# Moving a modulation product to GpSimd and casts ahead of a gelu in a one-core adaLN block

## The chip, the core and the metric

The kernel runs on one core of a Trainium2 chip. A core has five engines with queues of their own: TensorE (PE) multiplies matrices and writes to PSUM; VectorE (DVE) reduces and does arithmetic; ScalarE (ACT) applies functions; GpSimd (POOL) does arithmetic in SBUF; SyncE (SP) issues most DMAs. Each queue runs in the order in which it was written, and an instruction that waits holds up all behind it. The metric is the device time of one execution in microseconds (us).

## The reference

One transformer block for 2048 tokens of width 448 with 16 heads of width 28, in float32. A condition vector `c` gives six rows by one product: shift, scale and gate of the attention half (sa, ca, ga) and of the feed-forward half (sb, cb, gb).

```python
mod = (_silu(c) @ w_mod).reshape(c.shape[0], 6, 1, -1)
sa, ca, ga, sb, cb, gb = (mod[:, 0], mod[:, 1], mod[:, 2], mod[:, 3], mod[:, 4], mod[:, 5])
h = _layernorm(x, axis=-1) * (1 + ca) + sa
x = x + ga * _A_ref(h, A_wqkv, A_wo)      # softmax attention, 16 heads
h = _layernorm(x, axis=-1) * (1 + cb) + sb
x = x + gb * _B_ref(h, B_w1, B_b1, B_w2, B_b2)   # layernorm, 448 -> 1792, gelu, 1792 -> 448
return x
```

`w_mod` has 448 rows and 2688 columns, six parts of 448. The first part of the product below means sa and ca, the second ga, sb, cb and gb.

## The kernel before

**Numbers as two parts.** Most matrix products split each operand into a rounded part (`hi`, type fp32r) and the rest (`lo`), and add three products. Getting the pair takes a cast and a subtraction.

**Three stages.** The *projections* (to about 168 us) form Q, K and V for four blocks (`b`) of 512 tokens, normalise the next block meanwhile, and take the first row maxima of the attention scores. *Attention* runs 16 units: four head groups `g` of four heads by four query blocks `qt`, unit `u = 4 g + qt`. A unit has 16 steps, one for each 128 keys, and a step is 12 score matmuls (line 1382), two exponentials of 128 x 1024 on ACT (line 1395) and four matmuls with V of the step before (line 1337). The *feed-forward* part runs 14 steps `i` for each of four blocks, each with 11 matmuls of the first layer, a gelu, the split of its result, and 12 matmuls of the second layer for the step two back (`LAG`).

**Row maxima.** Before a unit begins, the maximum of each score row over all keys must be known. Single matmuls (line 476) put 128 x 512 scores in PSUM, and DVE reduces them (line 481). They are woven into the steps of earlier units by a plan made when the program is built. Before step `RING` = 121 a step has 3 to 5 such matmuls. From there on a step has one single, in the PSUM tile called `m1`, and one pair in a tile of two banks that DVE reduces at once (line 686). Before step 121 maxima over two key blocks can also be paired in another way: POOL forms the difference of two K blocks (`make_kd`, tile `d0h`); at the end of an odd step `open_pair` multiplies by it, ACT applies Relu, and in the next step `close_pair` adds the scores of the first block and takes the maximum in one DVE operation. `load_hi` loads a K or Q block of the next head group as soon as the last maximum that reads the old one is planned. When both blocks of a pair are issued, it plans `make_kd` for four steps later, and pairs may open from one step after that.

**The second part of the modulation.** `mod_load` brings four chunks of `w_mod` (128 or 64 rows, 1792 columns) into the slots of V blocks 2 and 3; `mod_mm` multiplies each by silu(c), broadcast to 32 columns, in block 1's first four projection tasks (line 752), so that each of the four rows lies 32 times in one PSUM tile. `mod_fin` copies it with three ACT operations, adds 1 to the third quarter (cb), sends four rows to DRAM and reads each back, broadcast to 128 partitions. The row ga scales `wo`, whose preparation (`wo_prep`, five items) runs at steps 0 to 16; the first product with it stands at step 216.

**The end of a unit.** `unit_end_tasks` sends the denominators through DRAM, multiplies on POOL (line 1062), casts `hi` (line 1072, DVE for 13 units), subtracts on POOL (line 1073) and stores both parts in DRAM. `max_fin` closes a set of maxima; POOL clears 16 columns of its tile each time (line 517).

**Seams of the feed-forward part.** Between blocks the rows of the next block, turned through DRAM (`send`, `fetch`), are cast to `hi` by ACT (line 1192) and subtracted by DVE (line 1193), four chunks each. They are written behind the whole first-layer step `i` = 13, that is behind its gelu (line 1428), the split of its result and two weight items. The seven tiles of a block rotate over eight buffers.

Of the kernel before, what the change touches and what calls it, by code (L numbers as in the profile page):

```python
# [13 lines left out]
F32 = mybir.dt.float32  # L14
# [8 lines left out]
D = 448  # L23
H = 16
DH = 28
# [7 lines left out]
P1RATE = 4  # L33
LAST_MAX = NKT - 4
RING = 121
PAIR_AT = (2, 2, 0, 2)
PAIR_ROWS = {(0, 2): 2, (0, 3): 3, (1, 0): 2, (1, 1): 2, (1, 2): 3}
WO_MAX = 3
# [6 lines left out]
def tile_adaln_block(ctx: ExitStack, tc: tile.TileContext, x, wqkv, wo, w1, b1, w2, b2, c, w_mod, out):  # L45
# [33 lines left out]
    def sbt(tag, shape, dt=F32, bufs=1):  # L79
        return sb.tile(shape, dt, tag=tag, name=nm(tag), bufs=bufs)  # L80
# [40 lines left out]

    ident = sbt("ident", [128, 128])
    make_identity(nc, ident)
    cst = sbt("cst", [128, 5])
    neg_half, zero_col = cst[:, 0:4], cst[:, 4:5]
    pool.memset(neg_half, -0.5)
    pool.memset(zero_col, 0.0)


    cols = sbt("cols", [128, 2 * NC])  # L130
# [183 lines left out]
    pc = ps_o()  # L314
    pe.transpose(pc[:, :NC], c_rows, ident[:NC, :NC])
    act.activation(sil_b, pc[:, :NC, None].broadcast_to([128, NC, 32]), AF.Silu)
    warm_up(5)
    for k in range(NC):
        for j in range(2):
# [183 lines left out]
    def load_hi(kind, g, b):  # L503
        loaded[(kind, g, b)] = clock[0] + (5 if clock[0] >= RING else 3)
        tg = ("kh" if kind else "qh") + str(b)
        t = sb.tile([128, 512], F32R, tag=tg, name=nm(tg), bufs=1)
        (kh_sb if kind else qh_sb)[(g, b)] = t
        sp.dma_start(f(t), f(dscr[kind][0][g])[:, b * 512 : (b + 1) * 512])
        if kind and b in (PAIR_AT[g], PAIR_AT[g] + 1) and all((g, PAIR_AT[g] + c) in kh_sb for c in range(2)):
            at(clock[0] + 4, lambda: make_kd(g))  # L510

    late = []


    def max_fin(g, qt):
        m32 = sbt("m32", [128, 32], F32R, bufs=2)
        pool.memset(f(m32)[:, 16:32], 0.0)
        dve.tensor_reduce(
            out=m32[:, 0:16].rearrange("p (h i) -> p h i", i=4),
            in_=mxp[(g, qt)].rearrange("p i h c -> p h i c"), op=ALU.max, axis=AX.X, negate=True,  # L520
        )
# [217 lines left out]

    mod = {}  # L740

    def mod_load(k):
        mod[k] = slot(f"v{2 + k % 2}", [128, 4 * D], F32)
        load_mod(mod[k], k, 2 * D, 4)

    def mod_mm(k):
        if k == 0:
            mod["p"] = ps_o()
        p = mod["p"]
        for j in range(4):  # L750
            rs_, cs = mod_part(k, j, 4)
            pe.matmul(
                p[32 * j : 32 * j + 32, :D], sil_b[rs_, k, :], mod[k][rs_, cs],
                start=(k == 0), stop=(k == NC - 1),
            )

    def mod_fin():
        t = sbt("full", [128, 512], bufs=3)
        act.copy(t[0:64, :D], mod["p"][0:64, :D])
        act.activation(t[64:96, :D], mod["p"][64:96, :D], AF.Identity, bias=1.0)  # L760
        act.copy(t[96:128, :D], mod["p"][96:128, :D])
# [56 lines left out]
    for b in range(NB):  # L818
# [12 lines left out]
        for n, (tb, kind, g) in enumerate(tasks):  # L831
# [41 lines left out]
                    later[n - 7](None)  # L873
            if n == (4 if b else 6):
                v_init(b)
            if b == 0 and n == 6:
                mod_load(0)
                mod_load(1)
# [4 lines left out]
            if b == 1:  # L883
                if n < 2:
                    mod_mm(n)
                    mod_load(2 + n)
                elif n in (2, 3):
                    mod_mm(n)
                    if n == 3:
                        mod_fin()  # L890
            if not more:
                if n == 0:
                    load_q(0)
# [68 lines left out]
    def wo_item(n):  # L962
# [11 lines left out]
        def go(r):  # L974
            full = sbt("full", [128, 512], bufs=3)
            ps = slice(0, 112 if n == 3 else 128)
            pool.tensor_tensor(out=full[ps, :D], in0=r[ps, :D], in1=rows["ga"][ps], op=ALU.mult)

            def rest():
                if n == 3:  # L980
                    hi = sbt("hi", [128, 512], F32R, bufs=3)
                    dve.tensor_copy(hi[ps, :D], full[ps, :D])
                    pool.tensor_tensor(out=wo_p[1][ps, 2, :], in0=full[ps, :D], in1=f(hi)[ps, :D], op=ALU.subtract)
                    pool.tensor_copy(wo_p[1][0:32, 2, :], f(hi)[0:32, :D])
# [6 lines left out]
            at(6 + 2 * n, rest)  # L991

        return ld, go

# [44 lines left out]
    def unit_end_tasks(u, o_sb):  # L1039
# [24 lines left out]
        def t_split2():  # L1064
# [7 lines left out]
            (dve.tensor_copy if staged else act.copy)(hi, on)  # L1072
            pool.tensor_tensor(out=lo, in0=on, in1=f(hi), op=ALU.subtract)
            st["hi"], st["lo"] = hi, lo
            if staged:
# [176 lines left out]
        sched.setdefault(step, []).append(fn)  # L1252

    wo_prep = Prep([wo_item(n) for n in range(5)])
    at(0, lambda: wo_prep.load(2))
    for n in range(5):
        at(4 + 2 * n, wo_prep.step)

    def b2_load():
        rows["b2"] = raw_t()  # L1260
# [13 lines left out]
        at(1 + i, lambda: put_spare(1))  # L1274
    for g in (1, 2):
        at(6 + g, lambda g=g: put_ones(g))
    at(15, b2_load)
    at(28, b2_mul)
    last0 = NKT * (NU - 1)
    lnst = [ln2_stages(b) for b in range(NB)]  # L1280
    for i in range(14):
# [133 lines left out]

    ov = out[0].rearrange("(b p t) n -> b p t n", p=128, t=4)

    def mlp1(b, i):
# [37 lines left out]
    def mlp2(b, m):  # L1456
# [18 lines left out]
        if m == NFT - 1:  # L1475
            for t in range(4):
                ot = xn_t()
                dve.tensor_tensor(out=ot[:, :D], in0=om[b][t][:, :D], in1=acc[b][:, t, :], op=ALU.add)
                sp.dma_start(ov[b][:, t, :], ot[:, :D])

    seq = [(b, i) for b in range(NB) for i in range(NFT)]
    for n in range(len(seq) + LAG):
        if n < len(seq):
            b, i = seq[n]
            if n:
                mlp1(b, i)
            for fn in tail.pop(n, ()):
                fn()
            for _ in range(2 if n % 2 else 1):
# [2 lines left out]
                lnst[b + 1][0](i)  # L1492
            if b:
                lnst[b][0](20 + i)
        ahead = n < len(seq) and i == NFT - 1 and b + 1 < NB
        if ahead:
            for k in range(2):
                lnst[b + 1][1](k)
        if n >= LAG:
            mlp2(*seq[n - LAG])  # L1500
        if ahead:
            for k in range(2, NC):
                lnst[b + 1][1](k)
    for key in ("t3", "t2", "t1", "t0", "m2", "m1", "o"):
        ps_close(key)

# [34 lines left out]
```

## Time and profile before

| | us |
|---|---|
| median of 3 runs | 1099.84 (1099.55 to 1100.01) |
| the profiled execution, its own time | 1099.75 |
| its span, from the first to the last instruction | 1097.5 |
| projections, to the first exponential of attention | 167.2 |
| a unit of attention, units 1 to 6 | 40 |
| a unit of attention, units 8 to 12 | 36 |
| a loop step of the feed-forward part | 5.0 |

A profile row gives start and duration in us, engine, line, operation, output and inputs, and in brackets the engine's idle time before it with what ended it. Rows of the grouped view give count, busy time in all, and the mean in ns. `PEld` is TensorE's weight load. Matmul ends are modelled, so starts are safer to compare than durations. The granted TensorE clock was 1.000 throughout.

### The profile page before, as it was taken

Reading aid. Unit: us, or ns where it says so; the run is one execution under the profiler, and the core shown is the slowest. Engines: PE = TensorE matmul, PEld = TensorE weight load, DVE = VectorE, ACT = ScalarE, POOL = GpSimd, SP = SyncE. Lnnn points to the kernel's source line nnn. Section 1 sums busy time; section 2 is a strip of 40 time slices with the busy share of each in tenths; the row PEclk is TensorE's granted clock in tenths of the full one; section 3 lists DMA queues with packets and bytes.
Section 4 is the critical chain, followed back from the end, with each engine's and each line's share of the span. In section 5 each row is a group of like instructions: output and inputs, shape, how many; then the busy total and the mean of one; then the engine's idle time right before and its main releaser. Section 6 shows DMA issues by size and latency. Waiting matters only on the chain.

```text
span 1097.5 us, 20709 instructions
## 1 busy us (share of the span) xinstructions
PE 1088.1 (99%) x8255; PEld 658.3 (60%) x8255; DVE 805.1 (73%) x1382; ACT 697.6 (64%) x883; POOL 198.7 (18%) x201
## 2 busy tenths in 40 slices
PE   8999999999999999999999999999999999999998
PEld 6756675444444444444444444554488788888887
DVE  6968788999999999988888888575655565463322
ACT  4565667888888888888888888678933411211211
POOL 1543332210000000000000000217123042061000
PEclk9999999999999999999999999999999999999999
DMA  9563354121222201232211213111442302002000
GB/s 312 207 190 103 97 188 134 59 65 32 72 76 64 77 28 41 67 98 54 69 48 38 86 49 104 58 31 59 136 137 65 101 34 55 18 34 72 34 1 34
DMA packets 58438, 88.57 MB, mean 81 GB/s; under 512 B 13759, under 2 KB 25686, under 8 KB 58330
## 3 DMA queue, kind: packets, MB, share of 16 engines
q1 hardware_dynamic: 57858, 86.51, 26.3%
q8 instruction: 65, 1.06, 0.4%
q10 hardware_dynamic: 148, 0.46, 0.1%
q0 software_dynamic: 336, 0.28, 0.1%
q14 instruction: 31, 0.25, 0.1%
HBM read 59.39 MB, written 29.50 MB: 81 GB/s over the span
## 4 chain that ended last, share of the span: by engine, by line
PE 96%; DVE 2%; DMA 1%; ACT 1%; issue 0%; SPq 0%; DVEq 0%; ACTq 0%
PE s L1382 23%; PE o L1337 23%; PE m L396 16%; PE pa L396 9%; PE m L476 8%; PE s L1472 3%; PE s L1473 3%; PE s L1474 3%; PE s L476 2%; PE t L1473 1%; PE t L1474 1%; PE t L1472 1%; DVE y L1193 1%; DMA slot_c<-in_w_mod_dram 1%; PE o L277 1%; DVE mxp L481 0%
## 5 line engine op out<-in xcount | busy, mean ns | idle before, releaser
L481 DVE TENSOR_REDUCE mxp<-m 128x1 f32<-128x512 f32 x555 | 359.7, 685 | 65.0 <-PE m L476 49.6
L1382 PE MATMUL s<-slot_b,slot_a 28*128 28x512 f32 (+1 forms) x3072 | 356.7, 423 | 0.0
L1382 PEld LDWEIGHTS s<-slot_b,slot_a 28*128 28x128 f32 (+1 forms) x3072 | 211.1, 183 | 176.0 <-ACT slot_c L1395 96.4
L476 PE MATMUL m<-kh,qh 28*128 28x512 f32 x607 | 226.9, 468 | 0.5 <-DVE mxp L481 0.3
L1395 ACT ACTIVATE slot_c<-s 128x1024 f32<-128x1024 f32 x170 | 174.7, 1028 | 51.6 <-PE s L1382 50.8
L1337 PE MATMUL o<-slot_c,v 128*32 128x512 f32 x680 | 178.9, 605 | 0.0
L1428 ACT ACTIVATE full<-m,b_col 128x512 f32<-128x512 f32 x56 | 38.6, 689 | 206.6 <-PE m L396 201.4
L686 DVE TENSOR_REDUCE mxp<-s 128x2 f32<-128x1024 f32 x107 | 131.1, 1226 | 5.1
L1337 PE MATMUL o<-slot_c1h,v 128*32 128x512 f32 x512 | 134.7, 605 | 0.0
L1337 PE MATMUL o<-slot_c0h,v 128*32 128x512 f32 x508 | 133.6, 605 | 0.0
L1395 ACT ACTIVATE slot_c1h<-s 128x1024 f32<-128x1024 f32 x128 | 130.7, 1021 | 0.0
L1395 ACT ACTIVATE slot_c0h<-s 128x1024 f32<-128x1024 f32 x127 | 130.5, 1028 | 0.0
L1395 ACT ACTIVATE slot_d<-s 128x1024 f32<-128x1024 f32 x86 | 88.4, 1028 | 25.0 <-PE s L1382 24.7
L1431 DVE CAST hi<-full 128x512 fp32r<-128x512 f32 x42 | 18.7, 444 | 112.3 <-ACT full L1428 112.3
L476 PEld LDWEIGHTS m<-kh,qh 28*128 28x128 f32 x607 | 90.7, 182 | 15.2 <-DVE mxp L481 13.1
L1337 PE MATMUL o<-slot_d,v 128*32 128x512 f32 x344 | 90.5, 605 | 0.4 <-ACT osb L1301 0.4
L1062 POOL TENSOR_TENSOR osb<-osb,osb 128x512 f32<-128x512 f32 x16 | 20.6, 1286 | 362.8 <-DMA osb<-drec 343.5
L1432 DVE TENSOR_TENSOR lo<-full,hi 128x512 fp32r<-128x512 f32 x56 | 46.0, 822 | 29.7 <-ACT hi L1431 25.1
L396 PE MATMUL m<-y,slot_a 128*128 128x512 f32 x160 | 60.9, 397 | 0.4 <-DVE y L1193 0.2
L481 DVE TENSOR_REDUCE mxp<-ma 128x1 f32<-128x512 f32 x61 | 39.5, 681 | 13.2 <-PE m L476 9.2
L1337 PEld LDWEIGHTS o<-slot_c,v 128*32 128x32 f32 x680 | 24.5, 108 | 39.1 <-issue 36.5
L650 DVE CUSTOM_DVE_ANT_0 slot_d0i<-m,slot_d0i 128x512 f32<-128x512 f32 x54 | 37.3, 691 | 14.3 <-PE m L476 11.3
(351 smaller groups left out, 1824.2 us busy)
## 6 DMA issues: line engine op xcount, KB each, us to landing
slot_b<-d SPq DMA_DIRECT2D x32, 256.0 KB
slot_a<-d SPq DMA_DIRECT2D x32, 256.0 KB
d<-lo SPq DMA_DIRECT2D x28, 256.0 KB
d<-hi SPq DMA_DIRECT2D x16, 256.0 KB
osb<-drec SPq DMA_DIRECT2D x15, 256.0 KB
out_dram<-xn SPq DMA_DIRECT2D x16, 224.0 KB
raw<-in_B_w_dram SPq DMA_DIRECT2D x14, 224.0 KB
qh<-d SPq DMA_DIRECT2D x12, 256.0 KB
```

What stands on the lines that cost most here:

```text
L396: pe.matmul(p, a, b, start=(i == 0), stop=(i == len(terms) - 1))
L476: pe.matmul(m, qh_sb[(g, qt)][js, i * 128 : (i + 1) * 128], k[js, :], start=True, stop=True)
L481: dve.tensor_reduce(out=mxp[(g, qt)][:, i, j, cch : cch + 1], in_=m, op=ALU.max, axis=AX.X)
L686: dve.tensor_reduce(out=mxp[(g, qt)][:, i, j : j + 2, cch], in_=t, op=ALU.max, axis=AX.X)
L1337: pe.matmul(o[32 * j : 32 * j + 32, :], v_sb[kt // 4][:, kt % 4, 4 * g + j, :], p[j // 2][:, j % 2, :], start=(kt == 0), stop=(kt == NKT - 1),
L1382: pe.matmul(s2[:, jj, :], ks[rows_, kp, kc], qs[rows_, qp, :], start=(term == 0), stop=(term == 2))
L1395: act.activation(pt[hf], s2, AF.Exp, scale=SCALE)
L1428: act.activation(gf, p, AF.Gelu_apprx_tanh, bias=b1_col[:, i : i + 1])
L1432: dve.tensor_tensor(out=glo, in0=gf, in1=f(ghi), op=ALU.subtract)
L1472: pe.matmul(pp, ghi[:, ts], w_hi, start=(m == 0), stop=False)
L1473: pe.matmul(pp, ghi[:, ts], w_lo, start=False, stop=False)
L1474: pe.matmul(pp, glo[:, ts], w_hi, start=False, stop=(m == NFT - 1))
```

## The change

Five edits.

1. The second part of the modulation leaves the projections. From step 124 on, every five steps, a chunk of 896 columns of `w_mod` is loaded into slot `a2h`; two steps later POOL multiplies it by silu(c) as a column (`sil_c`) and, from the second chunk on, adds it to a running sum, in `b1h` for ga and sb and in `a3h` for cb and gb. At step 166 four matmuls with a column of ones sum over the partitions, and one ACT operation adds 1 to the third quarter through a bias column (`third`).
2. `wo_prep` moves from steps 0 to 16 to steps 174 to 188, and the preparation of b2 with it.
3. The `hi` cast at the end of 13 units goes from DVE to POOL.
4. `make_kd` is planned one step after the second load, no longer four. The tiles of `max_fin` are made and cleared once.
5. At a seam the four casts and subtractions stand between the matmuls and the gelu of step `i` = 13.

```diff
-            at(clock[0] + 4, lambda: make_kd(g))
+            at(clock[0] + 1, lambda: make_kd(g))
...
+    m32s = [sbt(f"m32_{i}", [128, 32], F32R) for i in range(2)]
+    for m32 in m32s:
+        pool.memset(f(m32)[:, 16:32], 0.0)
...
-    def mod_load(k):
-        mod[k] = slot(f"v{2 + k % 2}", [128, 4 * D], F32)
-        load_mod(mod[k], k, 2 * D, 4)
...
-    def mod_mm(k):
...
+    def mod_load(h, k):
+        rs_ = mod_rows(h, k)
+        mod["raw"] = slot("a2h", [128, 2 * D], F32)
+        c0 = 2 * D * (1 + h)
+        sp.dma_start(mod["raw"][rs_], w_mod[128 * k : min(128 * k + 128, D), c0 : c0 + 2 * D])
+
+    def mod_add(h, k):
...
+        col = sil_c[rs_, k : k + 1].broadcast_to([rs_.stop - rs_.start, 2 * D])
+        pool.tensor_tensor(out=raw if k else total, in0=raw, in1=col, op=ALU.mult)
+        if k:
+            pool.tensor_tensor(out=total, in0=total, in1=raw, op=ALU.add)
+
+    def mod_fin():
+        p = ps_mx()
+        ones_ = v_sb[0].rearrange("p t h d -> p (t h) d")[:, 0:32, DH]
         for j in range(4):
...
+                p[32 * j : 32 * j + 32, :D], ones_, mod[j // 2][:, j % 2 * D : (j % 2 + 1) * D], start=True, stop=True,
...
+        act.activation(t[:, :D], p[:, :D], AF.Identity, bias=third)
...
-            (dve.tensor_copy if staged else act.copy)(hi, on)
+            (pool.tensor_copy if staged else act.copy)(hi, on)
...
-    at(0, lambda: wo_prep.load(2))
+    for i in range(2 * NC):
+        h, k = divmod(i, NC)
+        at(MOD_AT + 5 * i, lambda h=h, k=k: mod_load(h, k))
+        at(MOD_AT + 5 * i + 2, lambda h=h, k=k: mod_add(h, k))
+    at(MOD_AT + 10 * NC + 2, mod_fin)
+    at(WO_AT - 4, lambda: wo_prep.load(2))
...
         mm_acc(p, [(w, y) for y, w in ts])
+        if mid:
+            mid()
...
+    def seam(b):
+        return lambda: [lnst[b][1](k) for k in range(NC)]
...
-                mlp1(b, i)
+                mlp1(b, i, seam(b + 1) if i == NFT - 1 and b + 1 < NB else None)
```

The built programs show how this moves instructions. First PE in the projections, block 1, around the first modulation group (`pa` is a projection's PSUM tile, `o` the modulation's, `m` a row maximum's). Before:

```order
L396 MATMUL pa_742<-slot_c0h_511,slot_a_19_124 128x512
L396 MATMUL pa_742<-slot_c0h_511,slot_a_18_123 128x512
L752 MATMUL o_761<-slot_v_116_523,slot_d_4_86 32x448 x4
L396 MATMUL pa_774<-slot_c_110_510,slot_a_20_125 128x512
L396 MATMUL pa_774<-slot_c_110_510,slot_a_22_127 128x512
```

With the change:

```order
L401 MATMUL pa_745<-slot_c0h_518,slot_a_20_126 128x512
L401 MATMUL pa_745<-slot_c0h_518,slot_a_19_125 128x512
L401 MATMUL pa_770<-slot_c_113_517,slot_a_21_127 128x512
L401 MATMUL pa_770<-slot_c_113_517,slot_a_23_129 128x512
L401 MATMUL pa_770<-slot_c0h_518,slot_a2h_128 128x512
```

The group between two projection tasks is gone, here and at three later tasks. Its successor stands on PE in unit 10, between the V matmuls of step 165 (`o`) and the scores of step 167 (`s`), with the change:

```order
L1346 MATMUL o_7765<-slot_c1h_7901,v_233 32x512 x2
L1346 MATMUL o_7765<-slot_d_1903_7900,v_233 32x512 x2
L772 MATMUL m_1915_7958<-slot_b1h_6666,v_232 32x448 x2
L772 MATMUL m_1915_7958<-slot_a3h_7318,v_232 32x448 x2
L1391 MATMUL s_1923_7976<-slot_b_1768_7280,slot_a_1583_6431 128x512 x2
L481 MATMUL m_1924_7979<-kh_1804_7426,qh_1375_5591 128x512
```

The four matmuls of line 772 write a tile of the kind that the row maximum of line 481, two score matmuls later, writes again. Last, ACT at the first seam, from the gelu of step `i` = 12 on (`full<-m` is a gelu, `y` a cast of the next block's rows, `slot_e` a weight cast). Before:

```order
L1428 ACTIVATE full_11624<-m_2696_11612,b_col_253 128x512
L1431 CAST hi_11626<-full_11624 128x512
L1242 CAST slot_e_2700_11630<-full_11631 128x448
L1428 ACTIVATE full_11659<-m_2702_11647,b_col_253 128x512
L1431 CAST hi_11661<-full_11659 128x512
L1242 CAST slot_e_2700_11630<-full_11665 128x448
L1192 CAST y_11669<-xn_11591 128x4x4x32
L1192 CAST y_11670<-xn_11593 128x4x4x32
L1192 CAST y_11671<-xn_11595 128x4x4x32
L1192 CAST y_11675<-xn_11597 128x4x4x32
```

With the change:

```order
L1439 ACTIVATE full_11609<-m_2690_11597,b_col_260 128x512
L1442 CAST hi_11611<-full_11609 128x512
L1246 CAST slot_e_2694_11615<-full_11616 128x448
L1196 CAST y_11644<-xn_11576 128x4x4x32
L1196 CAST y_11645<-xn_11578 128x4x4x32
L1196 CAST y_11646<-xn_11580 128x4x4x32
L1196 CAST y_11650<-xn_11582 128x4x4x32
L1439 ACTIVATE full_11659<-m_2696_11632,b_col_260 128x512
L1442 CAST hi_11661<-full_11659 128x512
L1246 CAST slot_e_2694_11615<-full_11665 128x448
```

The four casts have passed the last gelu, its cast and a weight cast. The subtractions on DVE pass the split of that gelu's result in the same way.

More of the change, by code (lines that the diff above doesn't have):

```diff
@@ L35 @@
 RING = 121
+MOD_AT = 124
+WO_AT = 178
 PAIR_AT = (2, 2, 0, 2)
@@ L123, in tile_adaln_block @@
     make_identity(nc, ident)
-    cst = sbt("cst", [128, 5])
-    neg_half, zero_col = cst[:, 0:4], cst[:, 4:5]
+    cst = sbt("cst", [128, 6])
+    neg_half, zero_col, third = cst[:, 0:4], cst[:, 4:5], cst[:, 5:6]
     pool.memset(neg_half, -0.5)
-    pool.memset(zero_col, 0.0)
+    pool.memset(cst[:, 4:6], 0.0)
+    pool.memset(third[64:96], 1.0)
+    sil_c = sbt("sil_c", [128, NC])
     cols = sbt("cols", [128, 2 * NC])
@@ L316, in tile_adaln_block @@
     act.activation(sil_b, pc[:, :NC, None].broadcast_to([128, NC, 32]), AF.Silu)
+    act.activation(sil_c, pc[:, :NC], AF.Silu)
     warm_up(5)
@@ L509, in load_hi @@
         if kind and b in (PAIR_AT[g], PAIR_AT[g] + 1) and all((g, PAIR_AT[g] + c) in kh_sb for c in range(2)):
-            at(clock[0] + 4, lambda: make_kd(g))
+            at(clock[0] + 1, lambda: make_kd(g))
     late = []
+    m32s = [sbt(f"m32_{i}", [128, 32], F32R) for i in range(2)]
+    for m32 in m32s:
+        pool.memset(f(m32)[:, 16:32], 0.0)
     def max_fin(g, qt):
-        m32 = sbt("m32", [128, 32], F32R, bufs=2)
-        pool.memset(f(m32)[:, 16:32], 0.0)
+        m32s.append(m32s.pop(0))
+        m32 = m32s[-1]
         dve.tensor_reduce(
@@ L989, in rest @@
                     pool.tensor_tensor(out=wo_p[1][:, k, :], in0=full[:, :D], in1=f(wo_p[0])[:, k, :], op=ALU.subtract)
-            at(6 + 2 * n, rest)
+            at(WO_AT + 2 + 2 * n, rest)
         return ld, go
@@ L1254, in tile_adaln_block @@
     wo_prep = Prep([wo_item(n) for n in range(5)])
-    at(0, lambda: wo_prep.load(2))
+    for i in range(2 * NC):
[4 more added lines that the diff above has]
+    at(WO_AT - 4, lambda: wo_prep.load(2))
     for n in range(5):
-        at(4 + 2 * n, wo_prep.step)
+        at(WO_AT + 2 * n, wo_prep.step)
     def b2_load():
@@ L1276, in tile_adaln_block @@
         at(6 + g, lambda g=g: put_ones(g))
-    at(15, b2_load)
-    at(28, b2_mul)
+    at(WO_AT + 11, b2_load)
+    at(WO_AT + 24, b2_mul)
     last0 = NKT * (NU - 1)
@@ L1494, in tile_adaln_block @@
                 lnst[b][0](20 + i)
[L1495 to L1498, printed above, removed]
         if n >= LAG:
             mlp2(*seq[n - LAG])
-        if ahead:
-            for k in range(2, NC):
-                lnst[b + 1][1](k)
     for key in ("t3", "t2", "t1", "t0", "m2", "m1", "o"):
```

27 lines of the change are left out of this document (6 added, 21 removed).

## The prediction

> **What bounds the kernel now.** First the page's busy line and its chain of waits:
>
> ```profile
> PE 1088.1 (99%) x8255; PEld 658.3 (60%) x8255; DVE 805.1 (73%) x1382; ACT 697.6 (64%) x883; POOL 198.7 (18%) x201
> PE 96%; DVE 2%; DMA 1%; ACT 1%; issue 0%; SPq 0%; DVEq 0%; ACTq 0%
> ```
>
> TensorE (PE) is busy 99% and holds 96% of the chain that ended last. So an edit counts by the PE work that it adds or removes, and by the few places where PE waits. Then the view by windows (busy time of PE, weight loads, VectorE (DVE), ScalarE (ACT) and GpSimd (POOL) in a stretch, with the instructions of each; then clock, DMA share, GB/s):
>
> ```profile
> 60.00:75.00 15.00, 15.00 (x83) 8.45 (x80) 11.06 (x21) 8.59 (x17) 3.61 (x4) 1.00 0.73 226
> 209.00:249.00 40.00, 40.00 (x385) 18.42 (x381) 36.59 (x70) 33.91 (x39) 5.01 (x5) 1.00 0.26 73
> 488.00:524.00 36.00, 36.00 (x372) 15.58 (x368) 31.30 (x37) 31.52 (x34) 2.62 (x3) 1.00 0.22 62
> ```
>
> PE has no gap, neither in the projections (first row) nor in attention, whose units take about 40 us before step 121 and 36 us after it (second and third row). There DVE and ACT are near it, at 31 of 36 us or more: work put on them is not free. POOL has 33 of 36 us left.
>
> **Term 1: the modulation matmuls leave the projections.** The timeline shows four groups at line 752; here are the first and the last, each with PE's next work:
>
> ```profile
> 57.34 0.96 PE L752 MATMUL o<-slot_v,slot_d 128*32 128x448 f32 x8
> 58.23 1.20 PE L396 MATMUL pa<-slot_c,slot_a 128*128 128x512 f32 x4
> 71.89 0.96 PE L752 MATMUL o<-slot_v,slot_d 64*32 64x448 f32 x8
> 72.78 1.21 PE L396 MATMUL pa<-slot_c,slot_a 128*128 128x512 f32 x4
> ```
>
> Each group holds PE for 58.23 - 57.34 = 72.78 - 71.89 = 0.89 us, so 4 x 0.89 = 3.56 us go. Can DVE, which takes the row maxima behind PE, follow? Its first reduction behind each group, with its idle time in brackets:
>
> ```profile
> 60.11 1.89 DVE L481 TENSOR_REDUCE mxp<-m 128x1 f32<-128x512 f32 x3 [5.09 <-PE ma L476]
> 66.66 0.69 DVE L481 TENSOR_REDUCE mxp<-ma 128x1 f32<-128x512 f32 x1 [2.25 <-PE m L476]
> 69.53 1.29 DVE L481 TENSOR_REDUCE mxp<-ma 128x1 f32<-128x512 f32 x2 [0.38 <-PE m L476]
> 76.11 0.69 DVE L481 TENSOR_REDUCE mxp<-m 128x1 f32<-128x512 f32 x1 [2.29 <-PE ma L476]
> ```
>
> Behind the first, second and fourth group DVE was idle for longer than 0.89 us, so PE can come that much earlier; behind the third it had only 0.38 us to give. I take 3 x 0.89 + 0.38 = **-3.0 us**. Bounds: -1.9, if a third of it meets PSUM buffers that DVE has not emptied, and -4.0, if ScalarE, which loses three copies there, was holding PE too.
>
> **Term 2: the same sum inside attention.** It takes eight loads (steps 124 to 159), then on POOL eight multiplications and six additions of 896 columns, and at step 166 four matmuls and one ScalarE pass. The nearest rows:
>
> ```profile
> L1062 POOL TENSOR_TENSOR osb<-osb,osb 128x512 f32<-128x512 f32 x16 | 20.6, 1286 | 362.8 <-DMA osb<-drec 343.5 <-ACT slot_d L1395 19.4
> L1124 POOL TENSOR_TENSOR xn<-xn,row_cb 128x448 f32<-128x448 f32 x16 | 19.6, 1225 | 21.8 <-DVE xn L217 20.1 <-PE m L396 1.7
> 202.53 0.55 POOL L984 CAST slot_e<-hi 32x448 fp32r<-32x448 f32 x1
> L458 ACT COPY v<-pa 128x448 f32<-128x448 f32 x15 | 8.0, 534 | 3.6 <-PE pa L396 3.6
> ```
>
> 896 columns are twice 448, so an operation is 2.45 us and a stage at most 4.9 us. Stages come every 5 steps of 36/16 = 2.25 us, which is 11.25 us; a unit end's own three operations (1.29 + 0.63 for the cast, scaled from 448 to 512 columns, + 1.29 = 3.2 us) fit in as well. The last load is issued at step 159 and the matmuls stand at 166, 15.75 us later; with some 5 us for the load (an estimate: 0.23 MB, at the 62 GB/s and more of these stretches) and 4.9 us on POOL about 6 us are spare, so PE does not wait for the sum. PE pays 0.89 us for four matmuls like a group of line 752, and up to 0.5 us because the next row maximum needs the same PSUM tile (m1), which the ScalarE pass (0.53 us) must have read. I take **+1.2 us**; bounds +0.5 (DVE and ScalarE, on which PE leans here, catch up meanwhile) and +2.0 (the pass queues behind a whole exponential).
>
> The preparation of wo, now at steps 174 to 188, is first needed at step 216. Its five DVE casts fall where unit-end casts of the same size leave DVE: 0, and up to +0.5 us if each delays a maximum.
>
> **Term 3: unit-end cast and K difference, nothing.** The cast stood in line on DVE, and POOL waited for it:
>
> ```profile
> POOL lo L1073 <- DVE hi L1072: 93.1, 12, 9.7
> 242.69 0.82 SPq L508 DMA_DIRECT2D kh<-d  x2
> 247.22 1.28 POOL L611 TENSOR_TENSOR slot_d0h<-kh,kh 128x512 fp32r<-128x512 f32 x1 [6.03 <-PE s L1382]
> 248.06 0.50 PE L1382 MATMUL s<-slot_b,slot_a 29*128 29x512 f32 x2
> ```
>
> No unit waits for its result, which goes to DRAM; what hides the move is POOL's idle time. The K difference only moves which maxima are paired: 55 pairs for 54, with as many matmuls in nearly every step. Its risk is a difference that comes late, since PE opens the first pair of head group 1 at the end of step 31 instead of 35, and everything on PE queues behind it. The difference was ready at 247.22 + 1.28 = 248.50, and PE came to step 32 at 248.06: 0.4 us short. But the load stood behind the unit end's stores on SP's queue, and these leave earlier once POOL need not wait for the cast. I take 0; bounds 0 and +0.6.
>
> **Term 4: the seams.** In the chain, the first-layer matmuls of the feed-forward part start at:
>
> ```profile
> 865.56 2.56 PE m L396 x11
> 870.56 2.58 PE m L396 x11
> 882.74 2.56 PE m L396 x11
> 942.95 2.58 PE m L396 x11
> 953.34 2.56 PE m L396 x11
> 1013.57 2.58 PE m L396 x11
> 1023.96 2.55 PE m L396 x11
> ```
>
> A loop step is 870.56 - 865.56 = 5.00 us. Across the three seams two steps take 12.18, 10.39 and 10.39 us instead of 10.0 to 10.02: 2.16 + 0.37 + 0.37 = 2.9 us lost. The casts of the next block's rows stand behind the last gelu, its own cast and a weight cast. The change puts them ahead, where ScalarE is idle until that gelu's matmuls end; each new tile takes the buffer of an old one that these matmuls have just left, so the last cast ends about when they do. The gelu's result is wanted by PE two groups later, so a short delay of it costs nothing. At the first seam the rows' fetch may hold the casts:
>
> ```profile
> 869.08 2.42 SPq L1152 DMA_DIRECT2D xn<-y_dr  x5
> 874.00:874.50 0.50, 0.50 (x4) 0.47 (x3) 0.00 (x0) 0.50 (x1) 0.00 (x0) 1.00 0.28 82
> 874.50:875.00 0.50, 0.50 (x4) 0.46 (x3) 0.46 (x1) 0.01 (x1) 0.00 (x0) 1.00 0.00 0
> 876.27 2.18 ACT L1192 CAST y<-xn 128x512 fp32r<-128x512 f32 x4
> 876.94 0.50 PE L396 MATMUL m<-y,slot_b 128*128 128x512 f32 x1 [1.36 <-ACT y L1192]
> ```
>
> The DMA engines fall silent before 874.5, and PE wants the first tile at 870.56 + 5.00 = 875.6. I take **-2.7 us**; bounds -2.9, and -0.7 if the rows could not be used before 876.27, where the casts began.
>
> **Sum.** -3.0 + 1.2 + 0 - 2.7 = -4.5 us. The profiled execution took 1099.75 us, of which 1097.5 are the span, and the median of the runs is 1099.84: I predict **1095.3 us**.
>
> **Rivals.**
> 1. *The maxima hold the projections* (15%). DVE and five PSUM tiles set the pace, and term 1 gives only 0.4. For it speaks the 0.38 us of idle time behind the third group, against it the 2.25 and 2.29 us behind others. 1095.3 + 2.6 = 1097.9.
> 2. *The seam's rows are late* (9%). The first seam gives 2.0 less: 1097.3. For it speaks that only 1.1 us lie between silent DMA engines and PE's need, against it that the tiles land one after another.
> 3. *POOL blocks DVE in units 7 to 10* (9%); this is the slower end. In the feed-forward part a DVE subtraction from SBUF takes 1.46 us beside a POOL operation, and 0.69 alone:
>
> ```profile
> 901.73 1.46 DVE L1432 TENSOR_TENSOR lo<-full,hi 128x512 fp32r<-128x512 f32 x1
> 941.85 0.69 DVE L1432 TENSOR_TENSOR lo<-full,hi 128x512 fp32r<-128x512 f32 x1
> 541.32 1.30 POOL L1062 TENSOR_TENSOR osb<-osb,osb 128x512 f32<-128x512 f32 x1 [25.34 <-DMA osb<-drec]
> 541.47 0.69 DVE L481 TENSOR_REDUCE mxp<-m 128x1 f32<-128x512 f32 x1 [0.24 <-PE m L476]
> 542.20 0.22 DVE L518 TENSOR_REDUCE m<-mxp 128x16 fp32r<-128x64 f32 x1
> 542.33 1.22 DVE L686 TENSOR_REDUCE mxp<-s 128x2 f32<-128x1024 f32 x1
> ```
>
> In each of some 3.3 units DVE has four small operations from SBUF (a reciprocal, a memset, a reduction, a transposition). One could wait up to 2.45 us, less the 2.25 - 1.22 - 0.69 = 0.34 us that a step leaves, and POOL works 4.9 of 11.25 us: 3.3 x 4 x 2.1 x 0.44 = 12 us, so 1107. It decides from about 0.4 us of blocking on. Against it: beside POOL both the maxima, which read PSUM, and the small reduction kept their lengths. The Trainium skill (SBUF — State Buffer, "SBUF: two separate sides") states that GpSimd and a VectorE operation in a two-port mode or with two SBUF inputs take one pair of ports as an exclusive lock. The subtraction's rows agree with that rule; by it the maxima go free, and the sum stays.
> 4. *POOL's sum is late for its matmuls* (3%). If load and sums take 10 us longer than worked out, PE waits 4: 1099.3. Only the POOL time that was scaled up speaks for it.
>
> **Chances and range.** The forecast has 64%. Measurements of this kernel tell about 0.2% (2.2 us) from no change, so faster means under 1097.6 and slower over 1102.0. The forecast (but for 0.01), and some two thirds of the second and half of the first rival are faster, which makes 0.77; the rest of these and the fourth are no change, 0.14; the third is slower, 0.09. The bounds of the terms add up to -4.0 + 0.5 - 2.9 = -6.4 us at the good end, and -1.9 + 2.0 + 0.5 + 0.6 - 0.7 = +0.5 at the bad one, which needs all at once; I cut it where the first two rivals are inside: 1093.3 to 1098.6.
>
> **What would show it.** Right: no modulation matmuls between 57 and 72 us and attention beginning some 3 us earlier; attention units still of 40.0 and 36.0 us, but once 1 to 1.5 us more in unit 10; two loop steps of about 10.0 us over each seam. Wrong: projections as long as before, longer units 7 to 10, a wait of PE at step 31 or 166, or first-layer matmuls that still wait for the casts.

## The result and the profile after

The changed kernel takes **1094.09 us** (median of 4 runs, 1093.38 to 1094.88), the kernel before 1099.92 beside it: a ratio of 0.9944, with a 95% interval of 0.9932 to 0.9956. The forecast was 1095.3 us (1093.3 to 1098.6). The profiled execution took 1094.19 us, of which 1092.4 are the span, 5.1 less than before. Measured once more, later, the kernel gave 1094.13 us beside 1100.74, a ratio of 0.9942 (0.9929 to 0.9955).

Lines have new numbers: single maxima stand at line 481 (476 before), their reduction at 486 (481), the scores at 1391 (1382), the exponentials at 1404 (1395), the first layer of the feed-forward part at 401 (396). First the page's busy line and its chain of waits, of the changed kernel:

```profile
PE 1083.7 (99%) x8231; PEld 658.3 (60%) x8231; DVE 800.6 (73%) x1369; ACT 697.1 (64%) x883; POOL 231.9 (21%) x215
PE 96%; DMA 2%; DVE 1%; ACT 1%; issue 0%; SPq 0%; ACTq 0%
```

PE lost 4.4 us of work and is as full as before. POOL does 33 us more, VectorE has the thirteen casts less. What PE waited for (in all, times, longest, in us), the first row before:

```profile
PE m L396 <- ACT y L1192: 1.4, 1, 1.4
```

and the longest row of this kind that is new after:

```profile
PE m L481 <- ACT full L776: 0.3, 1, 0.3
```

PE's longest wait, the seam's, is gone from these rows, and a short new one stands behind the modulation's ScalarE pass in unit 10.

**Stages.** Since PE is busy 99% of the span, the lengths of the stages tell where the time went. A unit is measured from its first exponential to the next unit's, in the timeline of ScalarE. For unit 10, before:

```profile
559.92 1.02 ACT L1395 ACTIVATE slot_c<-s 128x1024 f32<-128x1024 f32 x1 [0.33 <-PE s L1382]
595.87 1.02 ACT L1395 ACTIVATE slot_c<-s 128x1024 f32<-128x1024 f32 x1 [0.35 <-PE s L1382]
```

and after:

```profile
555.99 1.03 ACT L1404 ACTIVATE slot_c<-s 128x1024 f32<-128x1024 f32 x1 [0.35 <-PE s L1391]
593.30 1.03 ACT L1404 ACTIVATE slot_c<-s 128x1024 f32<-128x1024 f32 x1 [0.30 <-PE s L1391]
```

595.87 - 559.92 = 35.95 us have become 593.30 - 555.99 = 37.31. All stages in that way; a seam is the two loop steps over it, and the projections run from block 1's first matmul to the first exponential:

| stage | before | after | difference | forecast | after, second profile |
|---|---|---|---|---|---|
| projections from block 1 | 118.25 | 114.84 | -3.41 | -3.0 | 114.77 |
| units 1 to 7 | 279.08 | 278.47 | -0.61 | 0 | 278.60 |
| units 8 and 9 | 71.94 | 71.99 | +0.05 | 0 | 72.01 |
| unit 10 | 35.95 | 37.31 | +1.36 | +1.2 | 37.34 |
| units 11 to 13 | 117.22 | 117.47 | +0.25 | 0 | 117.32 |
| unit 14 | 44.70 | 44.07 | -0.63 | 0 | 44.07 |
| first seam | 12.18 | 10.58 | -1.60 | -2.0 | 10.24 |
| second and third seam | 20.76 | 19.98 | -0.78 | -0.7 | 19.98 |
| behind the third seam | 73.71 | 73.93 | +0.22 | 0 | 73.86 |

These add up to -5.15; what lies ahead of block 1, unit 0, unit 15 and the steps between the seams moved by 0.07 us or less each. The rows below tell how each came about.

**Projections.** The first reductions behind the places where the groups stood, in VectorE's timeline, which answer to the four rows of the prediction:

```profile
59.08 1.89 DVE L486 TENSOR_REDUCE mxp<-m 128x1 f32<-128x512 f32 x3 [3.98 <-PE m L481]
64.78 0.69 DVE L486 TENSOR_REDUCE mxp<-ma 128x1 f32<-128x512 f32 x1 [1.42 <-PE m L481]
67.19 1.28 DVE L486 TENSOR_REDUCE mxp<-ma 128x1 f32<-128x512 f32 x2
72.83 0.69 DVE L486 TENSOR_REDUCE mxp<-m 128x1 f32<-128x512 f32 x1 [1.36 <-PE ma L481]
```

VectorE's idle time went from 5.09 to 3.98, from 2.25 to 1.42, from 0.38 to none and from 2.29 to 1.36: 1.11 + 0.83 + 0.38 + 0.93 = 3.25 us. What was to be given was given, and behind the third group VectorE is now the one that PE cannot outrun.

**Unit 10.** PE, ScalarE and VectorE around the modulation's matmuls:

```profile
570.63 0.55 PE L772 MATMUL m<-slot_b1h,v 128*32 128x448 f32 x2
571.50 0.50 PE L1391 MATMUL s<-slot_b,slot_a 29*128 29x512 f32 x2
571.63 0.63 ACT L776 ACTIVATE full<-m,cst 128x448 f32<-128x448 f32 x1 [0.22 <-PE m L772]
572.32 0.49 PE L481 MATMUL m<-kh,qh 28*128 28x512 f32 x1 [0.32 <-ACT full L776]
572.85 0.69 DVE L486 TENSOR_REDUCE mxp<-m 128x1 f32<-128x512 f32 x1 [1.92 <-PE m L481]
```

Four matmuls hold PE for 571.50 - 570.63 = 0.87 us; the single maximum of step 167 then waits for the ScalarE pass that reads its tile. VectorE meanwhile has no maxima for 1.92 us.

**POOL in units 7 to 10.** A multiplication of the sum (line 764) and its last addition (line 766):

```profile
503.29 1.68 POOL L764 TENSOR_TENSOR slot_a2h<-slot_a2h,sil_c 128x896 f32<-128x896 f32 x1 [11.28 <-DMA slot_a2h<-in_w_mod_dram]
...
556.87 2.12 POOL L766 TENSOR_TENSOR slot_a3h<-slot_a3h,slot_a2h 64x896 f32<-64x896 f32 x1
```

The sum is done at 558.99, 11.6 us ahead of its matmuls. And what VectorE did in 480 to 575 us meanwhile, grouped (count, busy us, mean ns, idle before); before:

```profile
L481 DVE TENSOR_REDUCE mxp<-m 128x1 f32<-128x512 f32 x42 | 29.0, 691 | 10.4 <-PE m L476 9.5 <-PE s L1382 0.6
L518 DVE TENSOR_REDUCE m<-mxp 128x16 fp32r<-128x64 f32 x2 | 0.4, 220 | 0.1
```

and after:

```profile
L486 DVE TENSOR_REDUCE mxp<-m 128x1 f32<-128x512 f32 x41 | 28.3, 691 | 12.3 <-PE m L481 10.9 <-PE s L1391 1.2
L525 DVE TENSOR_REDUCE m<-mxp 128x16 fp32r<-128x64 f32 x2 | 0.4, 220 | 0.1
```

No mean moved by a nanosecond, here or in the small operations left out: POOL's work takes nothing from VectorE here. Of the small operations that VectorE does on SBUF, a reduction of 0.22 us at 488.77 and a transposition of 0.20 us at 523.57 ran beside a multiplication of 896 columns (488.14 to 489.82 and 522.60 to 524.28) and kept their lengths; no reciprocal met one, so for that one this run shows nothing.

**First seam.** In the profiled execution PE still met late rows; ScalarE's casts, and the first matmul of step 13 and of the next block's step 1:

```profile
867.45 0.39 PE L401 MATMUL m<-y,slot_c 128*128 128x512 f32 x1
870.57 1.24 ACT L1196 CAST y<-xn 128x512 fp32r<-128x512 f32 x2 [1.34 <-DMA xn<-y_dr]
872.93 1.14 ACT L1196 CAST y<-xn 128x512 fp32r<-128x512 f32 x2 [1.12 <-DMA xn<-y_dr]
878.03 0.40 PE L401 MATMUL m<-y,slot_b 128*128 128x512 f32 x1
```

The casts no longer queue behind the gelu; two of them now wait for the fetched rows, 1.34 and 1.12 us, and the two steps take 878.03 - 867.45 = 10.58 us. The other two seams take 9.99 each.

### The profile page after: what moved, and what is told of

The parts are those of the page before. It is cut to its first block, busy times and chain, and to the rows that moved or that the text cites. A ratio compares the mean times of both kernels' runs of the same rounds, so it can differ in the third digit from the quotient of the medians.

```text
span 1092.4 us, 20666 instructions
## 1 busy us (share of the span) xinstructions
PE 1083.7 (99%) x8231; PEld 658.3 (60%) x8231; DVE 800.6 (73%) x1369; ACT 697.1 (64%) x883; POOL 231.9 (21%) x215
## 4 chain that ended last, share of the span: by engine, by line
PE 96%; DMA 2%; DVE 1%; ACT 1%; issue 0%; SPq 0%; ACTq 0%
PE o L1346 23%; PE s L1391 23%; PE m L401 16%; PE pa L401 9%; PE m L481 8%; PE s L1483 3%; PE s L1484 3%; PE s L1485 3%; PE s L481 2%; PE t L1484 1%; PE t L1485 1%; PE t L1483 1%; DMA slot_c<-in_w_mod_dram 1%; PE o L281 1%; DMA y_dr<-slot_e 1%; PE ma L481 0%
```

## The experiments

Ratios are to runs of the kernel before on the same chip in the same session, whose medians were 1100.49 (first four kernels), 1100.64 (next four) and 1100.74 us (last three). Differences of a few tenths are below what a ratio's interval resolves; there the lengths of stages decide, which among the profiles of kernels with the same work in a stage agree within about 0.2 us.

**1. The seams alone**: the kernel before with edit 5 only.

```diff
-        ahead = n < len(seq) and i == NFT - 1 and b + 1 < NB
-        if ahead:
-            for k in range(2):
-                lnst[b + 1][1](k)
...
+                mlp1(b, i, seam(b + 1) if i == NFT - 1 and b + 1 < NB else None)
```

> The kernel before with edit 5 alone (casts of the next block's rows ahead of the last gelu). Theory: the seams gain what they gained in the changed kernel, 1.6 us at the first and 0.37 us at each of the others, and nothing else moves: first exponential at 167.2 us, units 1 to 6 of 40.1 us, and the span 2.3 us under before's 1097.5, so 1095.2. Rival: the first seam's gain came in part from work that left the core's queues earlier (loads, wo preparation): then the first seam alone gains less than 1.2 us.

Measured: 1097.76 us, ratio 0.9976 (0.9967 to 0.9985). Its chain has the first-layer matmuls of step 13 and of the next block's step 1 at

```profile
872.71 2.56 PE m L396 x11
882.70 2.57 PE m L396 x11
```

so its two steps take 882.70 - 872.71 = 9.99 us, and so do the other seams: 2.97 us gained of 32.94. The first seam alone gains 2.19, more than the 1.6 expected, so the rival falls. Of the 2.97, 0.29 come back in this profile between the first and the second seam (60.50 us for 60.21), and the 2.7 that are left are what the medians differ by (1100.49 - 1097.76). Half of the change's gain or nearly so is this edit, and late rows are no necessary part of it.

**2. The K difference four steps behind its loads again**: the changed kernel with

```diff
-            at(clock[0] + 1, lambda: make_kd(g))
+            at(clock[0] + 4, lambda: make_kd(g))
```

> The changed kernel with the K difference planned four steps after its loads again. My prediction counted the K difference at nothing; the changed kernel's trace shows 0.6 us gone from units 1 to 7 and 0.6 us from unit 14, which nothing in my sum covers. Theory: both come from the order of the row maxima that the earlier difference makes; then this kernel is 1.0 to 1.3 us longer than the changed one (span about 1093.5) and unit 14 is 44.7 us again, not 44.1. Rival: they come from the cast and the cleared tiles that left DVE and POOL; then this kernel is as long as the changed one within 0.3 us.

Measured: 1095.18 us, ratio 0.995 (0.9934 to 0.9967); span 1094.2. Unit 14 takes 44.73 us, as before the change (44.70), and units 1 to 7 take 278.69 for 278.47. So the earlier difference is worth about 0.65 us in unit 14, where the last maxima are taken. For units 1 to 7 the theory is wrong: 0.2 of their 0.6 us came back, no more than profiles differ by. PE's single maxima in two of the steps there, in this kernel:

```profile
734.07 0.49 PE L481 MATMUL m<-kh,qh 28*128 28x512 f32 x1
734.40 0.39 PE L481 MATMUL m<-kh,qh 28*128 28x512 f32 x1
734.89 0.39 PE L481 MATMUL m<-kh,qh 28*128 28x512 f32 x1
738.85 0.50 PE L481 MATMUL m<-kh,qh 28*128 28x512 f32 x2
739.88 0.39 PE L481 MATMUL m<-kh,qh 28*128 28x512 f32 x1
```

and in the changed kernel:

```profile
732.39 0.50 PE L481 MATMUL m<-kh,qh 28*128 28x512 f32 x2
733.19 0.39 PE L481 MATMUL m<-kh,qh 28*128 28x512 f32 x1
736.96 0.50 PE L481 MATMUL m<-kh,qh 28*128 28x512 f32 x2
```

The first three rows are one step, the last two the next. One matmul less is left for the second of these steps, as 55 pairs in place of 54 leave one single fewer. In the first, two of three now start at the same moment (one row, x2) where they stood one behind the other; the step ahead of it shows the same. Each of three such steps is some 0.2 us shorter.

**3. The unit ends' cast on VectorE again**: the changed kernel with

```diff
-            (pool.tensor_copy if staged else act.copy)(hi, on)
+            (dve.tensor_copy if staged else act.copy)(hi, on)
```

> The changed kernel with the unit-end cast back on DVE. Theory: the cast costs PE nothing on either engine, the span stays within 0.3 us of the changed kernel's 1092.4; where it falls beside a multiplication or addition of 896 columns on POOL it takes 1 us or more instead of 0.42, and PE still does not wait. Rival (the third of the prediction, with an operation that can be blocked): units 7 to 10 become longer by 0.5 us or more each. Second rival: the 0.6 us that units 1 to 7 lost came from this cast; then they are 0.6 us longer here and kd_four shows nothing there.

Measured: 1095.64 us, ratio 0.9959 (0.9944 to 0.9974). Units 1 to 7 take 280.06 us, 1.6 more than with the cast on POOL, where the theory wanted no more than 0.3 in all; 0.9 of it lie in unit 1. Units 8 and 9 keep 72.02, so the first rival falls; the second has the place right and the size (0.6) too small. No cast took longer than 0.47 us, but none stood beside an operation of 896 columns, so what it would take there stays untried. SyncE's queue, POOL and PE in unit 1, at the stores of unit 0's result, in this kernel:

```profile
235.35 1.65 SPq L1087 DMA_DIRECT2D o<-hi  x4
235.41 1.28 POOL L1077 TENSOR_TENSOR lo<-osb,hi 128x512 fp32r<-128x512 f32 x1 [9.45 <-DVE mxp L478]
239.49 0.82 SPq L513 DMA_DIRECT2D kh<-d  x2
243.78 1.28 POOL L618 TENSOR_TENSOR slot_d0h<-kh,kh 128x512 fp32r<-128x512 f32 x1 [7.09 <-DMA kh<-d]
245.11 0.50 PE L481 MATMUL m<-slot_d0h,qh 28*128 28x512 f32 x1 [0.32 <-POOL slot_d0h L618]
```

and in the changed kernel:

```profile
226.77 1.63 SPq L1087 DMA_DIRECT2D o<-hi  x4
237.97 0.88 SPq L513 DMA_DIRECT2D kh<-d  x2
242.11 1.29 POOL L618 TENSOR_TENSOR slot_d0h<-kh,kh 128x512 fp32r<-128x512 f32 x1 [13.99 <-DMA kh<-d]
244.47 0.50 PE L481 MATMUL m<-slot_d0h,qh 28*128 28x512 f32 x1
```

With the cast on VectorE, POOL waits 9.45 us for that engine, the stores leave 8.6 us later, the K loads behind them on SyncE's queue 1.5 us later, and the difference is done at 245.06: PE waits. With the cast on POOL it is done at 243.40, 1.07 us ahead of its first matmul. These rows account for unit 1; the rest of the 1.6 us was not followed.

**4. The cast on VectorE and the late difference together**: both edits of 2 and 3.

> The changed kernel with both parts of edits 3 and 4 undone: the unit ends' cast on DVE, and the K difference planned four steps behind its loads (the tiles of max_fin stay made once). Theory (the cast on POOL is needed because of the earlier difference; with the later one no unit waits for it): the stalls at steps 29 to 32 that the cast on DVE brought (+1.6 us in units 1 to 7, 280.06 for 278.47) go, units 1 to 7 take 278.6 to 279.2 us, unit 14 takes 44.7, and the time is 0.4 to 1.0 us above the changed kernel's. Rival (the cast costs DVE time in units 1 to 7 of itself): they stay at 279.8 or more.

Measured: 1096.98 us, ratio 0.9962 (0.9948 to 0.9976), 2.85 above the changed kernel on the same chip (experiment 11), where 0.4 to 1.0 was expected. The stages do what the theory says: units 1 to 7 take 279.20 us (the rival wanted 279.8 or more), unit 14 takes 44.71. For units 1 to 7 there are now all four cases, one profile each:

| units 1 to 7, us | difference after 4 steps | after 1 step |
|---|---|---|
| cast on VectorE | 279.20 | 280.06 |
| cast on POOL | 278.69 | 278.47 |

The cast is worth 0.5 us by itself, and 1.6 with the early difference, which without it costs 0.9. The stages account for 0.6 + 0.15 (unit 10) + 0.64 = 1.4 of the 2.85. In the profiles, whose spans differ by 3.1, another 1.8 lie ahead of block 1's projections, where this kernel's first loads came later (PE waited 2.5 us for `w_mod` chunks, 1.5 in experiment 11). Whether the edits have a part in that was not tried.

**5 to 7. Modulation matmuls back in the projections**: the changed kernel with matmuls of the old shapes in block 1's tasks `n`, on data that lie in SBUF already, into a PSUM tile of the old kind that nothing reads. In 5 all four groups, in 6 the first alone, in 7 the third alone.

```diff
+            if b == 1 and n in (0, 1, 2, 3):
+                p = ps_o()
+                for j in range(4):
+                    rs_, _ = mod_part(n, j, 4)
+                    pe.matmul(p[32 * j : 32 * j + 32, :D], sil_b[rs_, n, :], acc[3][rs_, j, :], start=True, stop=True)
```

> The changed kernel with 16 matmuls of the old shapes put back at the four places of the projections, on resident data (x of block 3 and the broadcast silu), their result unused; no loads, no copies. Theory: PE time and DVE's room behind it made the whole gain of 3.3 us, so attention begins 3.0 to 3.4 us later than in the changed kernel (163.9 us), at about 167.1. Rival: the loads of 3.2 MB or the three ScalarE copies were worth 1 us or more; then attention begins at 166 us or earlier.

> The changed kernel with only the first of the four old matmul groups put back (resident data, result unused). Theory (DVE's idle time behind a group says what its removal gave): 0.89 us, so attention begins at 163.9 + 0.9 = 164.8 us. Rival (every group was worth the same share of 3.3 us, or the PSUM tiles decide): 0.8 us for both this and back_third, or none for either.

> The same with only the third group put back, behind which DVE had been idle for only 0.38 us. Theory: 0.4 us, attention begins at 164.3 us. Rival: 0.9 us like the first, at 164.8 us, in which case DVE's idle time behind one group does not bound what that group costs.

| | projections from block 1 | over 114.84 | time, us | ratio |
|---|---|---|---|---|
| all four | 118.13 | +3.29 | 1097.67 | 0.9974 (0.9965 to 0.9983) |
| the first | 115.86 | +1.02 | 1095.86 | 0.9956 (0.994 to 0.9972) |
| the third | 115.15 | +0.31 | 1094.85 | 0.995 (0.9934 to 0.9966) |

The matmuls alone, without their loads and without ScalarE's copies, bring back 3.29 of 3.41 us, the whole of it as far as profiles agree. One group costs three times another, as the theories of 6 and 7 forecast from VectorE's idle time, and equal shares are ruled out. VectorE's first reduction behind the first place, with the first group:

```profile
61.25 1.89 DVE L486 TENSOR_REDUCE mxp<-m 128x1 f32<-128x512 f32 x3 [5.09 <-PE m L481]
```

Behind the third place, with the third:

```profile
68.47 1.29 DVE L486 TENSOR_REDUCE mxp<-ma 128x1 f32<-128x512 f32 x2 [0.38 <-PE m L481]
```

The first group lengthens VectorE's idle time by 5.09 - 3.98 = 1.11 us, the third by 0.38: to the hundredth the idle times of the kernel before.

**8. Without the single maximum behind the modulation's matmuls**: the single of step 167 is left out there and taken later.

```diff
-                    if ring and (n, term) == ((1, 0) if late_one else (0, 0)) and not three:
+                    if ring and (n, term) == ((1, 0) if late_one else (0, 0)) and not three and step != MOD_AT + 10 * NC + 3:
```

> The changed kernel without the one row maximum of step 167, which uses the same PSUM tile (m1) as the modulation's sum; the maximum is planned later instead. Theory: PE pays 0.9 us for the four matmuls and 0.4 to 0.5 us for that tile, so unit 10 becomes 0.4 us shorter (36.9 us instead of 37.3), of which some 0.1 to 0.2 us come back where the maximum is taken. Rival: the rest above 0.89 us is the ScalarE pass of 0.63 us delaying the exponentials; then unit 10 stays at 37.3 us.

Measured: 1094.18 us, ratio 0.9941 (0.9926 to 0.9956). Unit 10 takes 36.64 us, 0.67 less; units 11 to 13 take 117.50, no less than in the changed kernel (117.47 and 117.32). That is more than the 0.4 expected, and the rival (37.3) falls. So of the 1.36 us, 0.69 go with the four matmuls and 0.67 with the maximum that follows. What leaving out another single of such a unit would gain was not tried, so the 0.67 need not be a conflict with the modulation. As a whole the time is the same within the interval.

**9. The same single half a step later**: behind the first two of the step's second six score matmuls.

```diff
-((1, 0) if late_one else (0, 0))
+((1, 0) if late_one or step == MOD_AT + 10 * NC + 3 else (0, 0))
```

> The changed kernel, with one single maximum of step 167 (in unit 10) half a step later, behind the first of the step's second six score matmuls instead of the first of its first six, so that ScalarE has read PSUM tile m1 (the sums of the modulation) before PE wants it again. Theory (0.3 to 0.7 us of unit 10 are PE's wait for that pass, and the single costs nothing elsewhere once it stays in its step): unit 10 takes 36.6 to 37.0 us for the changed kernel's 37.31, units 11 to 13 stay at 117.3 to 117.5, and the span is 0.3 to 0.7 us shorter than its own. Rival (the later single makes DVE late for the next pair): unit 10 keeps 37.3, or gives back what it gains in the two steps behind it.

Measured: 1094.62 us, ratio 0.9942 (0.9928 to 0.9956). Unit 10 takes 37.20 us, above the theory's 36.6 to 37.0 and near the rival's 37.3. VectorE and ScalarE behind the matmuls:

```profile
574.62 0.69 DVE L486 TENSOR_REDUCE mxp<-m 128x1 f32<-128x512 f32 x1 [1.90 <-PE s L481]
575.23 1.22 DVE L693 TENSOR_REDUCE mxp<-s 128x2 f32<-128x1024 f32 x1
576.55 0.69 DVE L486 TENSOR_REDUCE mxp<-m 128x1 f32<-128x512 f32 x1
576.98 1.02 ACT L1404 ACTIVATE slot_d<-s 128x1024 f32<-128x1024 f32 x1 [0.78 <-PE s L1391]
```

The single's matmul starts at 574.09 and no longer waits for the ScalarE pass, which ended at 574.04. But VectorE is idle for 1.90 us all the same, its next three reductions follow within 0.1 us of one another, and it is now ScalarE that waits 0.78 us for scores in step 168. The wait named in the profile was not the cost: with it gone, unit 10 is 0.11 us shorter. That VectorE's lost time is what counts fits with 8, where one reduction less gained what a reduction takes (0.69 us); shown is only that the named wait alone does not.

**10. The rows' fetch one stage earlier**: the changed kernel with block 1's turn, send and fetch a stage earlier (shown for the fetch).

```diff
-plan.setdefault(11 if b < 2 else 9, []).append(fetch)
+plan.setdefault(10 if b < 2 else 9, []).append(fetch)
```

> The changed kernel with block 1's turned rows sent one loop step earlier and fetched one step earlier, ahead of two weight loads on SP's queue. Theory: the first seam still loses 0.57 us because the fetch lands late; then its two steps take 10.0 us instead of 10.58, and the span falls by 0.5 to 0.6 us. Rival: the casts' own chain (four casts and subtractions) makes the loss; then nothing changes. Second rival: the weight loads that now stand behind the fetch come late, and a later step grows by as much.

Measured: 1097.32 us, ratio 0.9969 (0.9959 to 0.998). The first seam takes 9.99 us, and its four casts follow without a wait, but the steps ahead of it take 81.57 us in place of 79.24. Its chain of waits has, ahead of a first-layer step:

```profile
862.21 1.19 SPq L1215
863.44 2.69 DMA raw<-in_B_w_dram
```

The loads of the next weights (line 1215) now stand behind the send on SyncE's queue and leave at 862.21; in the changed kernel they leave ahead of it:

```profile
854.36 0.48 SPq L1215 DMA_DIRECT2D raw<-in_B_w_dram  x1
...
859.75 3.05 SPq L1146 DMA_DIRECT2D y_dr<-slot_e  x4
```

2.3 us are lost to gain 0.6 at most.

**11. The changed kernel once more.**

> The changed kernel once more, unaltered, as the reference for the two others on the same chip. By its first measurement: 0.993 to 0.996 of the time before, a span of 1091.6 to 1093.1 us, unit 10 at 37.3 us, units 1 to 7 at 278.5. Theory for the first seam (its casts wait for the fetched rows only when the transfers of an execution fall badly): it takes 10.0 to 10.6 us here, nearer to 10.0 as in five of the other runs. Rival (the wait belongs to the changed kernel): 10.58 again.

Measured: 1094.13 us, ratio 0.9942 (0.9929 to 0.9955), span 1092.3. The first seam took 10.24 us. In the profiles of kernels with the changed seam it took 9.96 to 10.58: the rows arrive about when they are wanted, and up to 0.6 us of the gain hang on it, 0.34 between two executions of the same kernel. But chance is not all of it. The fetch waits on SyncE's queue for the send to land in DRAM. Send and fetch with the seams alone (experiment 1):

```profile
864.85 3.04 SPq L1142 DMA_DIRECT2D y_dr<-slot_e  x4
871.23 2.42 SPq L1152 DMA_DIRECT2D xn<-y_dr  x5
```

and the fetch in the changed kernel, whose send left at 859.75 (experiment 10):

```profile
867.46 2.42 SPq L1156 DMA_DIRECT2D xn<-y_dr  x5
```

From send to fetch it is 6.38 us with the seams alone and 7.71 in the changed kernel. SyncE's wait for the send is 0.9 to 1.0 us in the kernel before and in experiments 1 and 5 to 7, and 1.9 to 2.3 us in the changed kernel, both times, and in experiments 2 to 4, 8 and 9. So the later landing goes with the kernel: those without modulation matmuls in the projections show it, those with them do not (10, which sends at another place, waits 0.9). Why is not known.

No version beats the changed kernel beyond the intervals.

## Why the prediction was right

It was right in sign, in the mechanism of the terms that make the sum (1, 2 in part, and 4) and, within 1.2 us, in size: -4.5 forecast, -5.8 by the first medians, -5.1 between the two profiles; the second medians say -6.6. That the maxima gain too was not foreseen. That the profiles come within 0.65 us is luck in part: units 1 to 7 and unit 14 gave 1.24 us that were put at nothing and the projections 0.41 more than forecast, while the first seam gave 0.40 less, units 10 to 13 cost 0.41 more and the end 0.22.

- **Term 1** (-3.0, measured -3.4). The reading of VectorE's idle time, 0.89 three times and 0.38 once, is borne out group by group (experiments 6 and 7). A group was worth 1.0 us where 0.89 was taken, the third 0.3 for 0.38; why a group costs 0.1 more than the distance from its start to the next task's start is not shown. The good bound's reason, copies that leave ScalarE, counts for some 0.1 at most (5 brings back all but that). The first rival, maxima that hold all of it, falls.
- **Term 2** (+1.2, measured +1.36 in unit 10). Four matmuls at 0.89 were right in the trace (0.87), and the 0.3 beside them stood for the conflict at tile `m1`. Experiments 8 and 9 give another split: some 0.7 go with the matmuls, 0.67 with the maximum behind them, and removing the wait for `m1` alone gains 0.1. So the 1.2 came out well, but not by the conflict that it was partly put on. The preparation of wo was put at 0 to 0.5; units 11 to 13 grew by 0.1 to 0.25.
- **Term 3** (0, measured -0.61 and -0.63). This is the step that was mis-sized, and its bound was on the wrong side: "bounds 0 and +0.6" left no room for a gain. It said that the difference "only moves which maxima are paired ... with as many matmuls in nearly every step". One single fewer in unit 14, and two that start together, are 0.65 us; the cast gave 0.5 in units 1 to 7. The risk that it named, a difference too late for the pairs, was real: it costs 0.9 us in the units where VectorE keeps the cast, and the stated rescue, stores that leave earlier when POOL need not wait for the cast, is what the rows of experiment 3 show.
- **Term 4** (-2.7, measured -2.4 in this profile, -2.97 in the seam alone). The mechanism is shown by experiment 1. The second rival, late rows, comes true in part, at 0 to 0.6 us for the 2.0 at which it was priced; what was not foreseen is that the send lands 1.2 us later in the changed kernel.
- **Rival 3**, POOL that blocks VectorE, falls: units 8 and 9 kept their 72 us while POOL's work went from 2.62 to 15.88 us in 488 to 524 us, no mean of VectorE moved, and the reduction and the transposition that ran beside a multiplication kept their lengths. The rule of the Trainium skill that was cited there (SBUF — State Buffer, "SBUF: two separate sides") left the maxima free, and the measured 691 ns before and after agree.
- **Rival 4**, a sum that comes late, falls: it was ready 11.6 us early. The operations took 1.68 (multiplication) and 2.11 us (addition) for the 2.45 scaled from 448 columns.

Small and open: 0.2 us behind the third seam, in all kernels with the whole change and not with the seams alone (73.68), and the 0.7 us by which the medians' difference exceeds that of the profiles, of which up to 0.6 can be the first seam. The start of an execution can be more: the profile of the kernel before has the earliest of all thirteen (48.97 us to block 1, for 49.04 to 51.17).

## What to carry to other kernels

When work leaves a full engine, read what the next engine in the chain idles behind that very instruction: here that idle time, place by place, told the cost of the two groups that were put back singly to 0.13 us (0.89 forecast and 1.02 measured, 0.38 and 0.31). A wait that the profile names can be worth less than its length (here 0.1 of 0.32 us); move it once before counting on it. Two edits that look free can hold each other up: the earlier K difference pays only with the stores freed by the cast (without that, 0.65 us gained in unit 14 and 0.9 lost in units 1 to 7).

## What the runs showed that was not expected

- An execution's start varies with its first loads: the same projections begin block 1 at 48.97 us in the profile of the kernel before and at 50.85 in that of the seams alone, which differ in nothing ahead of the feed-forward part. Stages measured from a point behind the loads agree within 0.1 us (118.25 and 118.28).
- On POOL a multiplication of 896 columns by a broadcast column takes 1.68 us, an addition of two tiles of that size 2.11 us, with 64 rows (1.68, and 2.09 and 2.12) as with 128.
- The number of single maxima is not all that they cost PE: two steps of unit 14 with the same three matmuls are 0.2 us shorter where two of them start together.
